# Moving one stretch of attention work by four matmuls, with its sums on VectorE in another order

## The chip, the cores and the metric

The kernel runs on one core of a Trainium2 chip. The metric is device time in microseconds (us) of one execution; lower is better. A core has TensorE (matrix products, PE in the profile; its weight loads are PEld), VectorE (DVE), ScalarE (ACT) and GpSimd (POOL), which each work through their own instructions in the order in which the program gives them, and SyncE (SP), on whose queue most DMA transfers are issued. The engines wait for one another through semaphores. TensorE writes only to PSUM, from where VectorE and ScalarE fetch its results.

## The reference

Retention (attention with a decay in place of the softmax) over 8 batches, 8 heads, 576 positions and 64 columns a head, and then a bilinear feed-forward layer on all 4608 tokens:

```python
scores = scale * np.matmul(q, k.transpose(0, 1, 3, 2))
Dmat = np.where(rel >= 0, gamma[:, None, None] ** rel[None, :, :], 0.0)
ret = scores * Dmat[None, :, :, :]
attn = np.matmul(ret, v)                       # (batch, head, position, 64)
x = attn.transpose(0, 2, 1, 3).reshape(B * S, H * D)   # 4608 x 512
a = x @ w_a                                    # 512 x 1536
b = x @ w_b
return (a * b @ w_out)                         # 4608 x 512
```

`rel` is query position minus key position, and `gamma` is one constant per head, so the decay factors into a power that belongs to the query and one that belongs to the key.

## The kernel before

**Attention as a recurrence.** The 576 positions of a batch are cut into nine blocks of 64. Within a block, the masked scores are multiplied with the values; what lies before the block comes through a state, the sum of key-times-value products of all earlier blocks. Most of the work is done in *pairs*: a pair is 256 positions (four blocks) of one batch, all heads. `PAIRS` lists them; the first eight are (batch 0, first 256), (1, first), (2, first), (0, second), (1, second), (2, second), (3, first), (3, second). The first three are made in another way at the start of the kernel (the `..._step` functions). The fourth pair has the number 3 and the fifth the number 4.

**A pair's steps.** `load_pair` (SP's queue) brings q, k and v. `ahead` (POOL) casts q and k to bf16 (`qkb`, L484 and L488) and multiplies v by the key's decay (`vb`, L495). `turn` (SP's queue, L507) transposes q and k by DMA into `qkT`. `stretch(into, outof)` then puts the products of two pairs on TensorE at one place:

- `open_outputs(outof)`: products of the states with the queries of pair `outof` into the PSUM tile `o` (L628), and a tiny ScalarE copy from `o` (`fence`, L671).
- `keyed(into, ...)`: keys times values of pair `into`, per block, into two PSUM tiles `kv` (L538).
- `matched(into)`: the scores of pair `into` into the PSUM tile `sc` (L600).
- `close_outputs(outof)`: masked scores times values, added into `o` (L641).

What follows these products on VectorE and ScalarE isn't issued on the spot. It is put into a list, `later`, as small entries:

- `add` (L560, L563, VectorE): the running sums of the blocks' `kv`, four in all. A pair whose number is in `SPLIT` has two entries of two sums each; any other pair has one entry with all four.
- `scaled` (L654, VectorE): the outputs times the query's decay, into `x`, two entries.
- `convert` and `convert_swapped` (ScalarE), each in one entry with half of the mask product `masked` (L609, VectorE): the sums become bf16 states (L570 for one block; L567 for the blocks whose halves are swapped, and, for the second pair of an odd batch, `left_states`).

**The feed-forward layer sets the order.** Tokens are taken in blocks of 512, 256, 256 and then 512. `ffn_block` runs, for each of the 12 parts F of the hidden width, four products into `pa` (L794), a ScalarE copy `ha` (L802), four products into `pb` (L809) and a VectorE product `hT` = ha x pb (L814). Then for each 128 tokens u it accumulates 12 products over F into an output tile `po` (L828), which is copied to `osb` (L837 on ScalarE in a block of 256 tokens) and stored. `pa`, `pb`, `po` and the `kv` tiles of a stretch share the tag "ab", which has four PSUM tiles.

`ffn_block` is a generator. After each product it yields that product's cost, where 512 columns count as 1, and whether other work may come in here (after each `hT`, after every fourth product of `po`, and after a `po` is copied). The loop at the end of the kernel adds the costs up and starts every entry of `todo` whose time has come:

```python
while todo and edge and at >= todo[0][0]:
    _, fn, args = todo.pop(0)
    fn(*args)
```

`ffn_block` also calls `pop()`, which issues the first entry of `later`: in a block of 256 tokens after each `hT`, after the products F = 2, 5 and 8 of a `po`, and after a `po` is copied. Whatever is left in `later` is issued by `flush()` at the end of a block, and at the start of the next stretch.

**Around the change.** The first block (512 tokens) counts 144 in all. The second, tokens 512 to 767, runs from 144 to 216: 48 for pa and pb, and 12 for each of its two output tiles. `stretch(3, None)` is due at 170 and `stretch(4, 3)`, with the scores of the fifth group and the outputs of the fourth, at 197. The third block, tokens 768 to 1023, reads the `x` that the fourth group's outputs give. At 200 and 200.1 to 200.3 `todo` also has `ahead(6)`, `turn(6)` and `load_pair(7)`. The buffers that pair 6 is cast and transposed into are those of pair 3 (three buffers each).

Of the kernel before, what the change touches and what calls it, by code (L numbers as in the profile page):

```python
# [18 lines left out]
def kernel(  # L19
# [25 lines left out]
    NP = NTOK // 256  # L45
    LEFT = {NP - 3: 0, NP - 1: 1}
    FIRST = 3
    SPLIT = (3, 5)
    assert S == 9 * 64 and B == 8

    PAIRS = [(0, 0), (1, 0), (2, 0), (0, 1), (1, 1), (2, 1)]
# [41 lines left out]
    def ps_next(name):  # L93

        opening.close()
        ps_o[0] = opening.enter_context(
            tc.tile_pool(name=name, bufs=1, space=PS))
# [179 lines left out]
    later = []  # L277
# [5 lines left out]
    def flush():  # L283
        while later:
            later.pop(0)()
# [235 lines left out]
    def keyed(n, alone):  # L521
# [64 lines left out]

        parts = [(0, 1), (2, 3)] if n in SPLIT else [(0, 1, 2, 3)]
        for part in parts:
# [3 lines left out]
    def matched(n):  # L592
        qkT = of(transposed, n)
        sc = ps_sc.tile([128, 2, HP, 2, 64], FP32, tag="sc", name="sc2")
        begun = Begun()
        for c in range(HP):
            for kp in (0, 1):
                for a, r in QUADS:
                    on = r ^ a
                    nc.tensor.matmul(sc[half(a), on, c, kp, :],  # L600
                                     qkT[half(on), 1, kp, c, half(a)],
                                     qkT[half(on), 0, kp, c, half(a)],
                                     start=begun.first(on, a), stop=True,
                                     skip_group_check=True)
        sT = st_pool.tile([128, 2, HP, 2, 64], BF16, tag="sT", name="sT2")
        scored[FIRST + n, "pair"] = sT

        def masked(on):
            nc.vector.tensor_tensor(  # L609
                sT[:, on].rearrange("p c k s -> p (c k) s"),  # L610
                sc[:, on].rearrange("p c k s -> p (c k) s"),
                mask3.unsqueeze(1).to_broadcast([128, 2 * HP, 64]),
                op=ALU.mult)
        return masked

    def from_states(n, o, begun):
        qkT = of(transposed, n)
        st = states_of.pop(n)
        first = first_of.pop(n, st[:, 0])
        for c in range(HP):  # L620
            for kp in (0, 1):
                for a, r in QUADS:
                    i = 2 * kp + a
                    if block_of(n, i) == 0:
                        continue
                    on = r ^ a
                    own = st[:, i] if i else first
                    nc.tensor.matmul(o[a][half(r), c, kp, :],  # L628
                                     own[half(on), c, :],
                                     qkT[half(on), 0, kp, c, half(a)],  # L630
                                     start=begun.first(a, r), stop=True,
                                     skip_group_check=True)

    def keys_into(n, o, begun):
        vb = of(natural, n)[1]
        sT = of(scored, n)
        for c in range(HP):
            for kp in (0, 1):
                for a, r in QUADS:
                    v0 = kp * DM + c * 128 + 64 * r  # L640
                    nc.tensor.matmul(o[half(r), a, c, kp, :],  # L641
                                     vb[half(a), v0:v0 + 64],
                                     sT[half(a), r ^ a, c, kp, :],
                                     start=begun.first(a, r), stop=True,
                                     skip_group_check=True)

    def scaling(n, o):

        s0 = 64 * block_of(n, 0)
        step = 0 if n in LEFT else 128  # L650

        def scaled(kp):
            t0 = place(n) * 256 + kp * 128
            nc.vector.tensor_tensor(  # L654
                x_of(t0, 128).rearrange("p c (a s) -> p c a s", a=2),
                o[:, :, :, kp].rearrange("p a c s -> p c a s"),
                qs[:, :, s0 + kp * step:s0 + kp * step + 128]
                .rearrange("p c (a s) -> p c a s", a=2),
                op=ALU.mult)
        return scaled  # L660
# [3 lines left out]
    def open_outputs(n):  # L664

        o = ps_o[0].tile([128, 2, HP, 2, 64], FP32, tag="o", name="o2")
        begun = Begun()
        from_states(n, [o[:, a] for a in (0, 1)], begun)

        kp = int(0 in (block_of(n, 0), block_of(n, 1)))  # L670
        nc.scalar.copy(fence, o[:, :, 0, kp, 0])  # L671
        opened[n] = o, begun

    def close_outputs(n):

        o, begun = opened.pop(n)
        keys_into(n, o, begun)
        scaled = scaling(n, o)
        later.append(lambda: scaled(0))
        later.append(lambda: scaled(1))  # L680
# [7 lines left out]
    def summing(n, own, of_keys):  # L688

        scaled = scaling(n, both.rearrange("p k a c s -> p a c k s"))  # L690

        def summed(kp):
            fresh = int(block_of(n, 2 * kp) == 0)
            for a in range(2):
                nc.scalar.copy(both[:, kp, a], of_keys[:, a, :, kp]
                               if a < fresh else own[a][:, :, kp])
            nc.vector.tensor_tensor(both[:, kp, fresh:], both[:, kp, fresh:],
                                    of_keys[:, fresh:, :, kp], op=ALU.add)
            scaled(kp)

        later.append(lambda: summed(0))
        later.append(lambda: summed(1))
# [11 lines left out]
    def stretch(into, outof):  # L714

        flush()
        if into == FIRST:
            ps_next("ps_pair")
        if into in LEFT:
            own = [ps_ffn.tile([128, HP, 2, 64], FP32, tag="ab", name=f"os{a}")  # L720
                   for a in (0, 1)]
            of_keys = ps_o[0].tile([128, 2, HP, 2, 64], FP32, tag="o",
                                   name="o2")
            from_states(outof, own, Begun())
            masked = matched(into)
            keys_into(outof, of_keys, Begun())
            summing(outof, own, of_keys)
            later.append(lambda: masked(0))
            later.append(lambda: masked(1))
            return  # L730
        if outof is not None:
            open_outputs(outof)
        convert, convert_swapped = keyed(into, outof is None)
        masked = matched(into)
        if outof is not None:
            close_outputs(outof)
        later.append(lambda: (convert(), masked(0)))
        later.append(lambda: (convert_swapped(), masked(1)))

# [244 lines left out]
    def third_turn():  # L984
        for i in (4, 5):
            transpose_step(i, (Q, "act"), (K, "dve"))

    todo = [(100, early_casts, ()),
            (112.1, cast_step, (5, Q, "act")),
            (124, third_turn, ()), (128, third_states, ()),  # L990
            (136, third_outputs, ())]
    todo += [(60 + 10 * n, total_of, (n,)) for n in (0, 1)]
    todo += [(136, total_of, (2,))]
    todo += [(28 + 6 * step, pair_tables, (step,)) for step in range(13)]
    todo += [(170, stretch, (3, None)), (197, stretch, (4, 3)),
             (252, stretch, (5, 4)), (274, open_alone, (5,)),
             (278, close_outputs, (5,)), (336, stretch, (6, None)),
             (372, stretch, (7, 6)), (408, stretch, (8, 7))]
    for n in range(8, NP, 2):
# [68 lines left out]
```

## Time and profile before

| what | value |
|---|---|
| median of 3 runs | 325.16 us (325.08 to 325.69) |
| the profiled execution | 325.43 us |
| its span in the profile | 323.7 us, 8631 instructions |
| granted TensorE clock | 1.00 |
| HBM read, written | 37.75 MB, 9.44 MB |
| chain that ended last | PE 92%, DMA 2%, SPq 2%, ACT 1%, issue 1%, DVE 1% |

A row of the time-ordered view gives the start in us from the beginning of the span, the duration, the engine, the line of the kernel, the operation, what it writes and reads, how many instructions are merged into the row, and in brackets how long the engine had been idle and what it had waited for. Matmul durations contain pipeline latency, so successive matmuls overlap; a few matmul records can be missing. "issue" is time in which an engine waited for nothing that the profile shows. The third block begins at 68.45 us, and the stretch of the change stands between 63.7 and 65.2 us.

### The profile page before, as it was taken

What the parts mean: (1) busy time and instruction counts of PE and PEld (TensorE: products, weight loads), DVE (VectorE), ACT (ScalarE), POOL (GpSimd) and SP (SyncE); (2) the same over time, 40 slices, a digit from 0 to 9 for tenths busy, and PEclk for the clock granted to TensorE, in tenths of its full rate; (3) what the DMA queues carried; (4) which work ended last, traced back from release to release, by engine and by line L of the source; (5) the groups of instructions that cost most, each with busy time, mean ns of one, the idle gap of its engine ahead of it and who ended that gap; (6) DMA issues with size and microseconds to landing.
All of it is one profiled execution on the core that took longest, in us unless ns stands there. A gap on an engine that the chain in (4) does not pass through costs nothing.

```text
span 323.7 us, 8631 instructions
## 1 busy us (share of the span) xinstructions
PE 314.0 (97%) x3573; PEld 164.4 (51%) x3611; DVE 165.4 (51%) x294; ACT 131.5 (41%) x293; POOL 118.8 (37%) x158
## 2 busy tenths in 40 slices
PE   7899999999999999999999999999999999999996
PEld 3564457778444554444454545454445444444444
DVE  5744445665546754835374626562566256514321
ACT  7735753463435523533253324442433343313321
POOL 4990077574755274447165305450530000000000
PEclk9999999999999999999999999999999999999999
DMA  8999999999999999999999169935840520031013
GB/s 216 255 196 207 259 231 189 200 176 206 174 221 223 195 208 206 269 222 263 175 197 216 52 163 198 207 74 144 194 86 19 104 76 2 2 97 32 1 23 108
DMA packets 145431, 50.90 MB, mean 157 GB/s; under 512 B 126704, under 2 KB 140912, under 8 KB 145392
## 3 DMA queue, kind: packets, MB, share of 16 engines
q1 hardware_dynamic: 140112, 45.37, 68.4%
q0 software_dynamic: 4752, 4.72, 8.8%
q8 instruction: 28, 0.46, 0.6%
q10 hardware_dynamic: 528, 0.26, 0.3%
q14 instruction: 11, 0.09, 0.1%
HBM read 37.75 MB, written 9.44 MB: 146 GB/s over the span
## 4 chain that ended last, share of the span: by engine, by line
PE 92%; DMA 2%; SPq 2%; ACT 1%; issue 1%; DVE 1%; DVEq 0%
PE pb L809 29%; PE po L828 29%; PE pa L794 28%; DMA qf<-in_q_dram 2%; SPq L159 2%; PE sc L600 1%; PE o L628 1%; PE o L641 1%; PE kv L538 1%; PE pa L771 1%; ACT state_after L386 0%; ACT vb L319 0%; PE tp L329 0%; DVE hT L814 0%; ACT own L390 0%
## 5 line engine op out<-in xcount | busy, mean ns | idle before, releaser
L814 DVE TENSOR_TENSOR hT<-ha,pb 128x512 bf16<-128x512 bf16 (+1 forms) x120 | 75.9, 633 | 94.8 <-PE pb L809 86.6
L802 ACT CAST ha<-pa 128x512 bf16<-128x512 f32 (+1 forms) x120 | 64.8, 543 | 115.9 <-PE pa L794 109.9
L809 PE MATMUL pb<-xT,wb_sb 128*128 128x512 bf16 (+1 forms) x474 | 111.2, 357 | 0.5
L794 PE MATMUL pa<-xT,wa_sb 128*128 128x512 bf16 (+1 forms) x452 | 106.9, 356 | 1.2 <-issue 0.6
L828 PE MATMUL po<-wo_sb,hT 128*128 128x512 bf16 (+2 forms) x442 | 94.7, 367 | 1.7 <-issue 1.4
L809 PEld LDWEIGHTS <-wb_sb 128*128 128x128 bf16 x480 | 47.0, 98 | 46.6 <-issue 0.3
L794 PEld LDWEIGHTS <-wa_sb 128*128 128x128 bf16 x468 | 45.0, 98 | 44.4 <-issue 0.2
L828 PEld LDWEIGHTS <-hT 128*128 128x128 bf16 x456 | 42.7, 98 | 47.2
L484 POOL CAST qkb<-qf 64x1024 bf16<-64x1024 f32 x15 | 15.5, 1031 | 64.4 <-DMA qf<-in_q_dram 55.1
L495 POOL TENSOR_TENSOR vb<-vf,vs 128x1024 bf16<-128x1024 f32 (+1 forms) x17 | 28.9, 1700 | 13.3 <-DMA vf<-in_v_dram 6.1
L839 DVE COPY osb<-po 128x512 f32<-128x512 f32 (+2 forms) x17 | 11.1, 653 | 43.0 <-PE po L828 43.0
L837 ACT COPY osb<-po 128x512 f32<-128x512 f32 (+1 forms) x21 | 12.0, 573 | 43.4 <-PE po L828 40.5
L484 POOL CAST qkb<-kf 64x1024 bf16<-64x1024 f32 (+1 forms) x17 | 16.4, 966 | 16.7 <-DMA kf<-in_k_dram 16.5
L563 DVE TENSOR_TENSOR sums<-kv,sums 128x256 f32<-128x256 f32 x44 | 18.7, 424 | 2.8 <-PE kv L538 0.8
L609 DVE TENSOR_TENSOR sT<-sc,mask 128x512 bf16<-128x512 f32 x30 | 19.4, 681 | 0.0
L488 POOL CAST qkb<-kf 64x512 bf16<-64x512 f32 (+1 forms) x34 | 18.7, 579 | 1.0
L488 POOL CAST qkb<-qf 64x512 bf16<-64x512 f32 x30 | 17.6, 615 | 0.6
L567 ACT CAST states<-sums 64x512 bf16<-64x512 f32 x26 | 16.0, 617 | 0.3
L654 DVE TENSOR_TENSOR xT<-o,qs 128x512 bf16<-128x512 f32 x24 | 15.4, 682 | 1.5 <-PE o L641 1.5
L311 POOL CAST qkb<-kf 128x512 bf16<-128x512 f32 x5 | 3.1, 617 | 16.9 <-DMA kf<-in_k_dram 16.9
L355 DVE TENSOR_TENSOR sT<-sc,mask_s 128x1024 bf16<-128x1024 f32 x6 | 7.2, 1222 | 1.3 <-PE sc L347 1.2
L855 PE MATMUL w<-ones 128*128 128x512 bf16 x17 | 6.3, 482 | 1.5 <-DVE idxp_f L204 1.5
(88 smaller groups left out, 163.5 us busy)
## 6 DMA issues: line engine op xcount, KB each, us to landing
qf<-in_q_dram SPq DMA_DIRECT2D x32, 256.0 KB, 4.7
vf<-in_v_dram SPq DMA_DIRECT2D x32, 256.0 KB, 5.2
kf<-in_k_dram SPq DMA_DIRECT2D x31, 256.0 KB, 4.8
out_dram<-osb SPq DMA_DIRECT2D x25, 256.0 KB, 3.2
out_dram<-osb SPq DMA_DIRECT2D x21, 128.0 KB, 2.6
wo_sb<-in_moe_w_out_dram POOLq DMA_DIRECT2D x3, 512.0 KB, 16.7
qf<-in_q_dram SPq DMA_DIRECT2D x8, 128.0 KB, 3.2
kf<-in_k_dram SPq DMA_DIRECT2D x8, 128.0 KB, 3.5
```

The costliest lines, as they stand in the source:

```text
L484: nc.gpsimd.tensor_copy(qkb[0:64, w, e], t[0:64, e])
L488: nc.gpsimd.tensor_copy(to[:, :, 1 - r], fro[:, :, r])
L495: nc.gpsimd.tensor_tensor(vb[:, e].rearrange("p (h d) -> p h d", d=D), t[:, e].rearrange("p (h d) -> p h d", d=D), decay[:, at], op=ALU.mult)
L563: nc.vector.tensor_tensor(sums[:, i], own, prev, op=ALU.add)
L567: nc.scalar.copy(to(half(1 - r)), fro(half(r)))
L609: nc.vector.tensor_tensor(sT[:, on].rearrange("p c k s -> p (c k) s"), sc[:, on].rearrange("p c k s -> p (c k) s"), mask3.unsqueeze(1).to_ ...
L654: nc.vector.tensor_tensor(x_of(t0, 128).rearrange("p c (a s) -> p c a s", a=2), o[:, :, :, kp].rearrange("p a c s -> p c a s"), qs[:, :, s ...
L794: nc.tensor.matmul(pa[:, 0:n], wa_sb[:, c, fs], xT[:, c], start=(c == 0), stop=(c == NC - 1))
L802: nc.scalar.copy(ha[:, 0:n], pa[:, 0:n])
L809: nc.tensor.matmul(pb[:, 0:n], wb_sb[:, c, fs], xT[:, c], start=(c == 0), stop=(c == NC - 1))
L814: nc.vector.tensor_tensor(hT[:, F, 0:n], has[F][:, 0:n], pb[:, 0:n], op=ALU.mult)
L828: nc.tensor.matmul(po[:, 0:width], hT[:, F, u * 128:(u + 1) * 128], wo_sb[:, F, cols], start=(F == 0), stop=(F == NF - 1))
```

## The change

`stretch(4, 3)` is due at 201 in place of 197, four products of 512 columns later. Pair 4 is added to `SPLIT`, so that its four state sums are two entries in place of one, and in that stretch the second of them is taken out of its place in the list and put behind the two `scaled` entries. `later` then reads: sums 0 and 1, scaled 0, scaled 1, sums 2 and 3, convert with half of the mask, convert_swapped with the other half. No instruction is added or left out.

```diff
-    SPLIT = (3, 5)
+    SPLIT = (3, 4, 5)
@@ stretch(into, outof)
         masked = matched(into)
         if outof is not None:
             close_outputs(outof)
+        if into == 4:
+            later.append(later.pop(1))
         later.append(lambda: (convert(), masked(0)))
         later.append(lambda: (convert_swapped(), masked(1)))
@@ todo
-    todo += [(170, stretch, (3, None)), (197, stretch, (4, 3)),
+    todo += [(170, stretch, (3, None)), (201, stretch, (4, 3)),
              (252, stretch, (5, 4)), (274, open_alone, (5,)),
```

## The prediction

> **What bounds the kernel now.** I began with the page's table of engines, then took the waits of TensorE from 60 to 130 us, and then the order-of-time view of TensorE, ScalarE and VectorE around the stretch that moves. In the first, TensorE (PE) is busy for 97% of the span. In the second, it waits there for no other engine: all that stands ahead of its matmuls is 0.7 us of "issue".
>
> ```profile
> PE 314.0 (97%) x3573; PEld 164.4 (51%) x3611; DVE 165.4 (51%) x294; ACT 131.5 (41%) x293; POOL 118.8 (37%) x158
> ```
>
> ```profile
> PE po L828 <- issue: 0.5, 3, 0.2
> PE pa L794 <- issue: 0.2, 1, 0.2
> ```
>
> So a delay of TensorE in this part goes to the end whole, and there is next to no wait here that a reordering could take away. Next, TensorE in order of time (start, duration, line, operation). The stretch is the rows before 65.21; the block of tokens 768 to 1023 begins at 68.45 with pa, pb, pa, pb, pa, 0.44 us each.
>
> ```profile
> 64.00 0.44 PE L538 MATMUL kv<-vb,qkb 64*64 64x64 bf16 x32
> ...
> 64.58 0.47 PE L641 MATMUL o<-sT,vb 64*64 64x64 bf16 x32
> 65.21 3.40 PE L828 MATMUL po<-wo_sb,hT 128*128 128x512 bf16 x15 [0.16 <-issue]
> 68.45 0.60 PE L794 MATMUL pa<-xT,wa_sb 128*128 128x256 bf16 x4
> 68.88 0.60 PE L809 MATMUL pb<-xT,wb_sb 128*128 128x256 bf16 x4
> 69.32 0.60 PE L794 MATMUL pa<-xT,wa_sb 128*128 128x256 bf16 x4
> 69.76 0.60 PE L809 MATMUL pb<-xT,wb_sb 128*128 128x256 bf16 x4
> 70.19 0.60 PE L794 MATMUL pa<-xT,wa_sb 128*128 128x256 bf16 x4
> ```
>
> The rows of ScalarE (ACT) and of VectorE (DVE) over the same time:
>
> ```profile
> 64.24 0.16 ACT L671 COPY fence<-o 128x2 f32<-128x2 f32 x1 [0.97 <-PE o L628]
> 66.06 0.59 ACT L837 COPY osb<-po 128x512 f32<-128x512 f32 x1 [1.66 <-PE po L828]
> 66.67 0.41 ACT L570 CAST states<-sums 128x256 bf16<-128x256 f32 x1
> 67.08 1.25 ACT L567 CAST states<-sums 64x512 bf16<-64x512 f32 x2
> 68.34 0.82 ACT L567 CAST left_states<-sums 64x256 bf16<-64x256 f32 x2
> 69.06 0.57 ACT L837 COPY osb<-po 128x512 f32<-128x512 f32 x1
> 69.54 0.84 ACT L802 CAST ha<-pa 128x256 bf16<-128x256 f32 x2
> ```
>
> ```profile
> 64.59 0.42 DVE L563 TENSOR_TENSOR sums<-kv,own 128x256 f32<-128x256 f32 x1 [0.87 <-PE kv L538]
> 65.12 1.34 DVE L563 TENSOR_TENSOR sums<-kv,sums 128x256 f32<-128x256 f32 x3
> 66.38 1.28 DVE L654 TENSOR_TENSOR xT<-o,qs 128x512 bf16<-128x512 f32 x2
> 67.58 1.28 DVE L609 TENSOR_TENSOR sT<-sc,mask 128x512 bf16<-128x512 f32 x2
> 69.94 0.95 DVE L814 TENSOR_TENSOR hT<-ha,pb 128x256 bf16<-128x256 bf16 x2 [1.08 <-PE pa L794]
> ```
>
> The reader is to see that ScalarE ran without a pause from 66.06 to 70.38. The state casts (L570, L567) lie between the copies of the two output tiles. The second copy starts at 69.06 though its matmuls were through by 68.65; the first ha cast is therefore late too, at 69.54, and ends at 69.91. The tag "ab" has four PSUM tiles. When the third pa starts at 70.19, the two pa and two pb before it hold all four, so it needs the first ha cast finished. It was, by 0.28 us.
>
> **Part 1, the place.** The schedule counts a product of 512 columns as 1. This block starts at 144, its twelve pa/pb pairs cost 48, its output tiles 12 each, and work is let in after every fourth product of a tile. So 197 is reached at 200, after eight products of the first tile, and 201 at 204, after its twelfth and its copy. A product takes (68.45 - 65.21) / 15 = 0.216 us, so on TensorE the four products come 0.86 us earlier and the stretch 0.86 us later. Its work is unchanged (129 small matmuls in 1.3 us in that window), and so is the gap beside it, since it follows a 512-column product both times: zero, with bounds of -0.58 us (both 0.42 us before its first load and 0.16 us after it vanish) and +0.58 us (one more of each).
>
> The eight moved-up products need their hT. The last hT of the block ends at 63.72 and its product would start at 64.27: covered by 0.55 us.
>
> **Part 2, the queue of small steps.** The list that the loop drains decides the rest. Before: sums, scale, scale, cast+mask, cast+mask, five entries; the five places left in the two tiles (one after the ninth product, one after the tile, three in the second) took them all. After: six entries (two sums, scale, scale, the other two sums, cast+mask, cast+mask), and only four places are left (three within the second tile and one behind its copy). They take the sums, the scales and the other sums. Both cast+mask entries go out at the block's end, behind the second tile's copy and ahead of the next block's first ha cast.
>
> **VectorE.** The first sum starts 0.86 later, 65.45; two sums at 0.45 end at 66.36; the scales run 66.38 to 67.66, just as before, as they need the last L641 product (65.05 + 0.86 = 65.91). So the next block's x is ready at 67.7 for 68.45. The other two sums end at 68.6 and the masks at 69.9. Both kv tiles come free at 68.1 and 68.6, ahead of the second pa at 69.32. Cost nothing; cover 0.75 us at x. If that went and x came at 68.6 (all four sums first), pa would start 0.15 us later, which the wait below swallows.
>
> **ScalarE.** The first tile's copy starts 0.41 us after its last product's start (65.64 to 66.06): now 64.27 + 0.41 = 64.68, ending at 65.27. The fence copy (0.16) comes behind it, to 65.43; the L641 products, which write the tile that it reads, are due at 64.58 + 0.86 = 65.44. Between 0 and 0.1 us of TensorE; I take 0.
>
> The second copy: its last product starts at 68.23, the copy at 68.65. Then, start to start as in the rows: copy to first cast 0.61, L570 0.41, the L567 pair 1.26, the left_states pair 0.72 to whatever follows. First ha cast at 68.65 + 3.00 = 71.65, done at 71.65 + 0.37 = 72.02, against 69.91 before. The third pa can start at about 72.06 instead of 70.19: **TensorE stands still for 1.87 us**. Behind it, the first hT product runs 72.05 to 72.47 and the fourth buffer turn (pb at 72.50) just fits; the next ones have 0.4 us to spare. So no second wait follows. TensorE never waits for a transfer or an engine from here to 130 us beyond issue, so nothing gives it back.
>
> [...] In the rows two casts of one kind follow each other without overlap (67.08 to 68.34 is 2 x 0.617 plus 0.02), and only at a change between casts and PSUM copies does one start 0.10 us early (68.34 + 0.82 = 69.16 against 69.06). [...]
>
> Bounds from rows: if all six starts were 0.10 early, durations of 0.59 + 0.41 + 1.23 + 0.81 = 3.04 less 0.60 give 2.44 and a wait of 1.31. If TensorE hid nothing, all 2.39 us of casts (66.67 to 69.06) plus 0.1 for the fence count: 2.5. I take 1.87, which is the same instructions in the same order.
>
> **Part 3, other queues.** Pair 6's casts (POOL) are now written ahead of the stretch, as are its transposes (SP), and the loads of pair 7. The stretch issues nothing on POOL or SP, so both queues keep their order. Casts and transposes reuse buffers that the stretch reads last, by 65.91. The casts start at 78.24 (their q loads are issued at 73.39, 4.7 us to landing), the transposes at 84.59: cover 12 us and 18 us. Zero; if it went, POOL, and SP with pair 7's v load behind the transposes, would start late by as much, and the first to feel it would be the score products that read pair 6 from 97.44.
>
> **Sum.** +1.87, taken as +1.9. The profiled execution took 325.43 us (span 323.7 and 1.7 around it), 0.27 over the median of 325.16. It becomes 327.3, the median 327.1.
>
> **Rivals.**
> *Casts in time (not slower).* The same list, but the cast entries reach ScalarE before the second tile's copy. To cost nothing the first ha cast must end by 70.15, so the casts must start by 67.4 rather than 69.26. For it: sums and data are ready (the sums that the first cast needs end at 66.36), and ScalarE idles from 65.4 to 68.6. Against it: no place is left to let them in, and in all rows ScalarE keeps the written order. Time 325.2, or 324.6 if the 0.58 us of issue goes as well.
> *The clock falls after the pause.* The first eight warm-up matmuls of 512 columns take 0.42 us each rather than 0.216:
>
> ```profile
> 1.52 3.34 PE L855 MATMUL w<-ones 128*128 128x512 bf16 x8 [1.52 <-DVE idxp_f L204]
> ```
>
> so TensorE can run at half rate after standing still, though the granted clock reads 1.00 there. If 1.9 us were enough, 3.3 us at half rate would cost 1.6 more: 328.7. Against it: after the 0.46 us wait at 11.42 the spacing is 0.21 again, but no pause between that and the launch is seen in the trace, so the rows leave the point open. [...]
>
> **How the numbers follow.** ScalarE's casts stall TensorE: 0.87, own range 326.4 to 327.9 (median plus 1.3 to 2.5, and 0.1 to 0.2 for the runs' spread). Casts in time: 0.08, of which 0.02 below 324.5. Clock falls: 0.05. 0.2%, 0.65 us, is about what a measurement can tell here. Slower 0.87 + 0.05 = 0.92; within 0.06; faster 0.02. The range 326.4 to 327.9 is the likeliest case's own; its tails and the other cases leave out about 0.2.
>
> **What would show it.** Right: the stretch's L628 follows the twelfth product; the second L837 copy at about 68.65, L570 and the L567 casts behind it, the first ha at 71.65; a wait of about 1.9 us ahead of the third pa on "ACT ha", and all later rows of TensorE that much later; scale rows (L654) unmoved at 66.4. Wrong: L567 rows ahead of the second L837, or ha at 69.5 (then no change); product spacing of 0.42 after the pause (then the clock); or a wait ahead of the first pa on "DVE xT" (then VectorE).

## The result and the profile after

The changed kernel takes 327.05 us in the median (326.81 to 327.35, 5 runs) against 325.16 (325.04 to 325.69, 5 runs): a ratio of 1.0057, with a 95% interval of 1.0043 to 1.0070. The ratios leave out slow executions, of which there is one here, the 332.67 us of `pause_half`. The change makes the kernel slower by 1.9 us, within 0.05 us of the forecast. The profiled execution took 327.35 us, with a span of 325.6 against 323.7.

The waits of TensorE in the changed kernel, between 60 and 130 us (who waited for whom: us in total, times, longest), have one entry that wasn't there before:

```profile
PE pa L796 <- ACT ha L804: 1.7, 1, 1.7
```

TensorE in order of time (start, duration, line; from line 737 on, lines stand two higher than in the kernel before):

```profile
61.92 2.75 PE L830 MATMUL po<-wo_sb,hT 128*128 128x512 bf16 x12
...
65.45 0.47 PE L641 MATMUL o<-sT,vb 64*64 64x64 bf16 x32
65.85 2.76 PE L830 MATMUL po<-wo_sb,hT 128*128 128x512 bf16 x12
68.45 0.60 PE L796 MATMUL pa<-xT,wa_sb 128*128 128x256 bf16 x4
68.89 0.60 PE L811 MATMUL pb<-xT,wb_sb 128*128 128x256 bf16 x4
69.33 0.60 PE L796 MATMUL pa<-xT,wa_sb 128*128 128x256 bf16 x4
69.76 0.60 PE L811 MATMUL pb<-xT,wb_sb 128*128 128x256 bf16 x4
72.07 0.60 PE L796 MATMUL pa<-xT,wa_sb 128*128 128x256 bf16 x4 [1.71 <-ACT ha L804]
72.50 0.60 PE L811 MATMUL pb<-xT,wb_sb 128*128 128x256 bf16 x4
```

The stretch now stands between two output tiles of twelve products each. The next block starts at 68.45, as before. Then the third pa starts at 72.07 in place of 70.19, 1.88 us late. The wait shows as 1.71 because it is counted from the modelled end of the last matmul. ScalarE over the same time:

```profile
64.71 0.59 ACT L839 COPY osb<-po 128x512 f32<-128x512 f32 x1 [1.43 <-PE po L830]
65.19 0.17 ACT L671 COPY fence<-o 128x2 f32<-128x2 f32 x1
68.66 0.59 ACT L839 COPY osb<-po 128x512 f32<-128x512 f32 x1 [3.30 <-PE po L830]
69.27 0.41 ACT L570 CAST states<-sums 128x256 bf16<-128x256 f32 x1
69.68 1.24 ACT L567 CAST states<-sums 64x512 bf16<-64x512 f32 x2
70.94 0.82 ACT L567 CAST left_states<-sums 64x256 bf16<-64x256 f32 x2
71.66 0.63 ACT L804 CAST ha<-pa 128x256 bf16<-128x256 f32 x2
```

ScalarE now idles for 3.3 us ahead of the second copy, and then has the state casts in front of the first ha cast, which moves from 69.54 to 71.66. VectorE did what the change asks of it:

```profile
65.46 0.42 DVE L563 TENSOR_TENSOR sums<-kv,own 128x256 f32<-128x256 f32 x1 [1.73 <-PE kv L538]
65.99 0.42 DVE L563 TENSOR_TENSOR sums<-kv,sums 128x256 f32<-128x256 f32 x1
66.33 1.28 DVE L654 TENSOR_TENSOR xT<-o,qs 128x512 bf16<-128x512 f32 x2
67.53 0.87 DVE L563 TENSOR_TENSOR sums<-kv,sums 128x256 f32<-128x256 f32 x2
```

The scales start at 66.33, where they stood before (66.38), so x is there for the first pa. The 1.9 us stay to the end: the later stretch whose first key products stood at 97.44 has them at 99.31.

### The profile page after: what moved, and what is told of

The parts are those of the page before. It is cut to its first block, busy times and chain, and to the rows that moved or that the text cites. A ratio compares the mean times of both kernels' runs of the same rounds, so it can differ in the third digit from the quotient of the medians.

```text
span 325.6 us, 8668 instructions
## 1 busy us (share of the span) xinstructions
PE 318.2 (98%) x3611; PEld 164.9 (51%) x3611; DVE 165.1 (51%) x294; ACT 131.5 (40%) x293; POOL 118.6 (36%) x158
## 4 chain that ended last, share of the span: by engine, by line
PE 93%; DMA 2%; SPq 2%; ACT 1%; issue 1%; DVE 1%; DVEq 0%
PE po L830 29%; PE pb L811 28%; PE pa L796 28%; DMA qf<-in_q_dram 2%; SPq L159 2%; PE sc L600 1%; PE o L641 1%; PE o L628 1%; PE kv L538 1%; PE pa L773 1%; PE o L437 0%; PE sc L347 0%; PE kv L374 0%; ACT states L567 0%; PE tp L329 0%
## 5 line engine op out<-in xcount | busy, mean ns | idle before, releaser
L796 PE MATMUL pa<-xT,wa_sb 128*128 128x512 bf16 (+1 forms) x468 | 108.8, 357 | 1.7 <-ACT ha L804 1.7
L830 PE MATMUL po<-wo_sb,hT 128*128 128x512 bf16 (+2 forms) x456 | 97.0, 368 | 0.0
L567 ACT CAST states<-sums 64x512 bf16<-64x512 f32 x26 | 16.0, 617 | 0.3
L857 PE MATMUL w<-ones 128*128 128x512 bf16 x19 | 7.2, 503 | 1.5 <-DVE idxp_f L204 1.5
```

The costliest lines, as they stand in the source:

```text
L567: nc.scalar.copy(to(half(1 - r)), fro(half(r)))
L796: nc.tensor.matmul(pa[:, 0:n], wa_sb[:, c, fs], xT[:, c], start=(c == 0), stop=(c == NC - 1))
L830: nc.tensor.matmul(po[:, 0:width], hT[:, F, u * 128:(u + 1) * 128], wo_sb[:, F, cols], start=(F == 0), stop=(F == NF - 1))
```

## The experiments

The theory: the whole loss is the state casts that ScalarE gets behind the second output tile's copy, since TensorE runs into the first ha cast when the four shared PSUM tiles are full. The rivals: the later place costs by itself (everything from the stretch on is 0.86 us late); the new order on VectorE costs; TensorE waits for something other than the tiles; or the clock falls after the pause. Differences below are medians against the kernel before in the same series (325.31, 325.18 and 325.10 us in the three series).

### One half of the change, and the other

The new order alone, at the old place:

```diff
-    todo += [(170, stretch, (3, None)), (201, stretch, (4, 3)),
+    todo += [(170, stretch, (3, None)), (197, stretch, (4, 3)),
```

> The changed kernel with the stretch back at 197: only the split sums and the new order on VectorE stay. Theory (what counts is which casts ScalarE gets behind the second output tile's copy): six entries for five places, so the swapped casts (1.26 + 0.72 us) go out at the block's end, behind the copy, while the L570 cast (0.41) still goes ahead of it. First ha cast at 68.66 + 0.60 + 1.26 + 0.72 = 71.24, done at 71.61, third pa at 71.65: +1.46 us, 326.6. Rival 'the later place itself costs' (everything 0.86 us late): as before, 325.2. Rival 'the new order on VectorE costs it all': as the changed kernel, 327.05.

Measured: 326.76 us, +1.45, ratio 1.0043 (1.0031 to 1.0055). ScalarE, in order of time (this execution runs 0.42 us earlier throughout than the one of the kernel before):

```profile
66.25 0.40 ACT L570 CAST states<-sums 128x256 bf16<-128x256 f32 x1
68.23 0.59 ACT L839 COPY osb<-po 128x512 f32<-128x512 f32 x1 [1.57 <-PE po L830]
68.84 1.24 ACT L567 CAST states<-sums 64x512 bf16<-64x512 f32 x2
70.09 0.82 ACT L567 CAST left_states<-sums 64x256 bf16<-64x256 f32 x2
70.82 0.63 ACT L804 CAST ha<-pa 128x256 bf16<-128x256 f32 x2
```

L570 slips in ahead of the copy, the L567 casts don't. With the place unchanged, three quarters of the 1.9 us are lost: six entries find only five places ahead of the second tile's copy, and the sixth, with the L567 casts, goes out behind it. This run holds the split and the new order together; that the sixth entry matters and not the order is read from the rows of ScalarE.

The new place alone, with the old entries and the old order:

```diff
-    todo += [(170, stretch, (3, None)), (197, stretch, (4, 3)),
+    todo += [(170, stretch, (3, None)), (201, stretch, (4, 3)),
```

> The kernel before with the stretch at 201: the old five entries and the old order on VectorE. Theory: five entries for four places; L570 goes out behind the second tile's copy and the swapped casts at the block's end, so ScalarE has the same rows as in the changed kernel and the first ha cast ends at 72.03. The four sums now stand ahead of the scales, x is ready at 68.53 instead of 67.6 and the first pa starts at about 68.57 instead of 68.45, which the later wait swallows: +1.9 us, 327.05. Rival 'VectorE's new order costs it': 325.2 to 325.3. Rival 'both waits add up': 327.2 or more.

Measured: 327.39 us, +2.1, ratio 1.0068 (1.0053 to 1.0082). The scales on VectorE, and then TensorE, in order of time:

```profile
67.26 1.28 DVE L654 TENSOR_TENSOR xT<-o,qs 128x512 bf16<-128x512 f32 x2
```

```profile
68.59 0.60 PE L794 MATMUL pa<-xT,wa_sb 128*128 128x256 bf16 x4
...
72.08 0.60 PE L794 MATMUL pa<-xT,wa_sb 128*128 128x256 bf16 x4 [1.58 <-ACT ha L802]
```

The first pa is 0.14 us late, right behind the scales that end at 68.54, and the third pa starts at 72.08, as in the changed kernel (72.07). The median alone would also fit the rival by which both waits add up (327.2 or more). The rows speak against it: the later stretch has its first key products at 99.32, against 99.31 in the changed kernel. So the delay of x is swallowed here, and the new order on VectorE gains nothing as long as ScalarE sets the time. The halves don't add up (1.45 and 2.1 against 1.9): both act through the same row, the first ha cast.

### The same place without the late casts

Here the six steps are joined so that all of them find a place within the second output tile. First with the new order on VectorE:

```diff
         if into == 4:
-            later.append(later.pop(1))
+            steps = [later[i] for i in (0, 2, 3, 1)]
+            later[:] = [lambda: (steps[0](), steps[1]()),
+                        lambda: (steps[2](), steps[3]()),
+                        lambda: (convert(), masked(0),
+                                 convert_swapped(), masked(1))]
+            return
```

> The changed kernel at 201 with its order on VectorE, but with the six steps joined into three entries (sums and first scale; second scale and sums; all casts and masks), so that all of it is let in within the second tile and ScalarE has the casts ahead of the second copy. Theory: the swapped casts now wait for the third sum (ends at about 67.97) and run from 68.0 to 70.0, the copy ends at 70.55, and the second pb, which needs the tile that this copy frees, waits from 69.76 to about 70.6: +0.85 us, 326.0, with the wait on the osb copy in place of the ha cast. Rival 'the later place itself costs': 327.05.

Measured: 326.15 us, +0.84, ratio 1.0027 (1.0018 to 1.0036). The wait has changed its place, as expected. The waits of TensorE, then ScalarE (this execution too runs about 0.35 us early):

```profile
PE pb L816 <- ACT osb L844: 0.7, 1, 0.7
```

```profile
66.10 0.41 ACT L570 CAST states<-sums 128x256 bf16<-128x256 f32 x1 [1.10 <-DVE sums L563]
67.63 1.25 ACT L567 CAST states<-sums 64x512 bf16<-64x512 f32 x2 [1.12 <-DVE sums L563]
68.89 0.82 ACT L567 CAST left_states<-sums 64x256 bf16<-64x256 f32 x2
69.61 0.57 ACT L844 COPY osb<-po 128x512 f32<-128x512 f32 x1
```

Now the scales stand in the way: the swapped casts wait 1.12 us for the sums that were put behind them, and push the copy back. Then with the four sums first, from the kernel before:

```diff
-    todo += [(170, stretch, (3, None)), (197, stretch, (4, 3)),
+    todo += [(170, stretch, (3, None)), (201, stretch, (4, 3)),
@@ stretch
+        if into == 4:
+            steps = list(later)
+            later[:] = [steps[0], lambda: (steps[1](), steps[2]()),
+                        lambda: (convert(), masked(0),
+                                 convert_swapped(), masked(1))]
+            return
```

> The stretch at 201, all four sums ahead of the scales as in the kernel before, and three entries (sums; both scales; all casts and masks), let in within the second tile. Theory: the third sum ends at about 66.87, the swapped casts run from 66.9 to 69.0 ahead of the second copy (68.9), the first ha cast ends at 69.75, the third pa finds its tile free. Only x is late, by 0.1 us at the first pa: +0.1 us, 325.3, no wait on ScalarE. Rival 'the later place itself costs': 326 or more.

Measured: 325.40 us, +0.09, ratio 1.0007 (0.9996 to 1.0017). There is no wait of TensorE in the view from 60 to 130 us, and ScalarE has its casts ahead of the copy again:

```profile
66.86 1.24 ACT L567 CAST states<-sums 64x512 bf16<-64x512 f32 x2
68.12 0.82 ACT L567 CAST left_states<-sums 64x256 bf16<-64x256 f32 x2
68.84 0.57 ACT L843 COPY osb<-po 128x512 f32<-128x512 f32 x1
69.32 0.36 ACT L808 CAST ha<-pa 128x256 bf16<-128x256 f32 x1
```

So the later place hardly costs anything by itself: with the same place, the same products and the casts ahead of the copy, 0.09 us of the loss is left (by the interval, at most 0.55), about what the late x was expected to cost. That rival has fallen.

### The casts later still

```diff
-        flush()
+        if tb != 1:
+            flush()
         tok += n
```

> The changed kernel without the flush at the end of the block of tokens 512 to 767: the two cast+mask entries stay in the list and are let in after the first and the second hT of the next block. Theory: ScalarE casts the first ha at 69.25, then L570, the second ha, the swapped casts (70.4 to 72.4) and only then the third ha, which ends at about 72.8; the fifth pa, which needs that tile, waits from 71.94 to about 72.8: +0.9 us, 326.1, no wait at the third pa. Rival 'the late casts cost the same wherever they stand': 327.05. Rival 'the later place itself costs': 327.05.

Measured: 326.17 us, +0.99, ratio 1.0028 (1.0016 to 1.0040). The third pa doesn't wait; the fifth does, behind the same casts (this execution runs 0.15 us early):

```profile
72.65 0.60 PE L796 MATMUL pa<-xT,wa_sb 128*128 128x256 bf16 x4 [0.70 <-ACT ha L804]
```

So the same casts cost half as much there. What they cost depends on which ha cast they stand in front of, and on the tiles that TensorE can still fill by then, not on their sum.

### More tiles

If TensorE stops because the four shared tiles are full, two more move the stop on by one pa and one pb. The first try takes the two halves of the idle output tile:

```diff
+                if tb == 2 and F == 2:
+                    extra = ps_o[0].tile([128, 2, 512], FP32, tag="o",
+                                         name="extra")
                 pa = (begun[F] if tb == 0 and F in begun else
+                      extra[:, 0] if tb == 2 and F == 2 else
...
+                pb = (extra[:, 1] if tb == 2 and F == 2 else
```

> The changed kernel, but in the block of tokens 768 to 1023 the third pa and the third pb take the two banks of the output tile o, which nothing uses from 67.6 us to the next stretch, in place of two of the four shared tiles. ScalarE's queue is unchanged, its first ha cast still ends at 72.03. Theory (TensorE stops because all four shared PSUM tiles are held until that cast): the third pa runs at 70.19 and the third pb at 70.63 without a wait, and the fourth pa is the one that waits, from 71.07 to 72.07: +1.0 us in place of +1.9, 326.2. Rival 'TensorE waits for ScalarE or the masks for another reason than the tiles' (the x, the hT buffer): the third pa still starts at 72.07, 327.05.

Measured: 327.28 us, +2.1, ratio 1.0061 (1.0046 to 1.0076): a miss by 1.1 us. TensorE, and then the ScalarE cast that it waits for, in order of time (about 0.36 us early throughout):

```profile
69.84 0.60 PE L800 MATMUL extra<-xT,wa_sb 128*128 128x256 bf16 x4
72.25 0.60 PE L816 MATMUL extra<-xT,wb_sb 128*128 128x256 bf16 x4 [1.81 <-ACT ha L808]
```

```profile
71.83 0.37 ACT L808 CAST ha<-extra 128x256 bf16<-128x256 f32 x1
```

The third pa ran without a wait, as the theory has it. But the third pb then waited for ScalarE's read of the other half of the same tile: the wait had only moved on. Why the write into one half waited 1.81 us for the read of the other no run shows. With two separate tiles:

```diff
+                if tb == 2 and F == 2:
+                    third_a = ps_o[0].tile([128, 2, 512], FP32, tag="o",
+                                           name="third_a")
+                    third_b = ps_sc.tile([128, 2, 512], FP32, tag="sc",
+                                         name="third_b")
...
+                      third_a[:, 0] if tb == 2 and F == 2 else
...
+                pb = (third_b[:, 0] if tb == 2 and F == 2 else
```

> The changed kernel with the third pa of the block of tokens 768 to 1023 in the output tile o and the third pb in the score tile sc, two tiles in place of the two halves of one (in fifth_tile the third pa did run without a wait, but the third pb waited for ScalarE's read of the other half). The score tile is read for the last time at 69.6. Theory (TensorE stops when the shared tiles are all held until the first ha cast at 72.03): the third pa and pb run at 70.19 and 70.63, the fourth pa waits from 71.07 to 72.07: +1.0 us, 326.2. Rival (something other than the number of free tiles holds the products back): 327.05 to 327.3.

Measured: 326.33 us, +1.2, ratio 1.0030 (1.0012 to 1.0048), where +1.0 was expected. TensorE, in order of time (about 0.2 us early):

```profile
70.44 0.60 PE L818 MATMUL third_b<-xT,wb_sb 128*128 128x256 bf16 x4
71.87 0.60 PE L802 MATMUL pa<-xT,wa_sb 128*128 128x256 bf16 x4 [0.84 <-ACT ha L810]
```

Both run without a wait, and the fourth pa would have started 0.44 us after the third pb, at 70.88; it is 0.99 us late, as expected of the tiles. ScalarE's queue has the same rows in the same order, so the number of free tiles is shown to set where TensorE stops.

### Does the clock fall after a pause?

The prediction had left open whether a pause of 1.9 us drops TensorE's clock. A pair of casts done again makes it longer, by 0.62 us (one of the pair again), 1.25 (the pair twice in all) or 3.75 (four times). The edit of `pause_1`; `pause_3` has 3 in place of 1, and `pause_half` one ScalarE copy in place of the loop:

```diff
             swapped(lambda r: odd_ones(into, r, 1),
                     lambda r: odd_ones(sums, r, 0))
+            for _ in range(1 if n == 4 else 0):
+                swapped(lambda r: odd_ones(into, r, 1),
+                        lambda r: odd_ones(sums, r, 0))
```

> The changed kernel with the pair of 64x512 casts of the swapped states done twice (the same values written again), 1.25 us more on ScalarE at that place. Theory: the third pa starts at 73.3, TensorE pauses for 3.0 us by the waits, 328.3. If the clock holds, the pa and pb after the pause take 0.44 us per four matmuls from the first on; rival 'the clock falls after a pause': 0.85 us per four for a while, and up to 1.6 us more, 329.9.

> As before, with the pair of casts done four times, 3.75 us more on ScalarE. Theory: the third pa starts at 75.8, TensorE pauses for 5.5 us, 330.8 if the clock holds. [...]

> The changed kernel with one of the two 64x512 casts of the swapped states done twice: 0.62 us more on ScalarE, a pause of TensorE of 2.3 us. If the clock holds through such a pause: 327.7 in all runs, granted clock 1.00. If it can fall there as in the runs of pause_1 with a granted clock of 0.99: some runs 1.2 us or more above 327.7.

> pause_1 once more, for the share of executions in which the clock falls after a pause of 3.0 us: 328.3 to 328.7 where the granted clock stays at 1.00, 329.8 and more where it reads 0.995 or less. [...]

The pause is that of the profiled execution.

| kernel | pause by the waits | median, ratio (95% interval) | execution times, with the granted clock over the span |
|---|---|---|---|
| changed | 1.7 us | 327.05, 1.0057 (1.0043 to 1.0070) | 326.81 to 327.35, all five at 0.999 to 1.00 |
| pause_half | 2.25 us | 329.75, 1.0108 (1.0068 to 1.0148) | 327.69 and 327.90 at 1.00; 329.57, 329.93, 330.00 at 0.995; 332.67 at 0.99 |
| pause_1 | 3.0 us | 329.92, 1.0150 (1.0111 to 1.0189) | 328.66 at 1.00; 329.82 and 330.01 at 0.995; 332.91 at 0.99 |
| pause_1_again | 3.0 us | 330.41, 1.0158 (1.0112 to 1.0205) | 328.69 and 329.32 at 1.00; 329.90 and 330.92 at 0.995; 331.98 and 333.09 at 0.99 |
| pause_3 | 5.6 us | 334.01, 1.0275 (1.0249 to 1.0301) | 333.66 to 334.08 at 0.99; 336.01 at 0.985 |

Where the clock held, pause_half meets its 327.7, and pause_1 and its repeat come within 0.4 us of the 328.3 that the longer queue gives, but for one execution of 329.32. Most executions lie above, and those have the lower clock. So four of six executions of pause_half took 1.8 us or more above 327.7, as in the second of its two cases, and in the repeat of pause_1 four of six lie at 329.8 or more, all with a clock of 0.995 or less, as its expectation has it for such a clock. pause_3 was 2.9 us or more above the 330.8 of a clock that holds. The windows of its profiled execution show the reason (stretch in us; length, and PE's busy time first, and the granted clock third from the end):

```profile
73.00:76.00 3.00, 0.00 (x0) 0.00 (x0) 0.00 (x0) 2.90 (x5) 0.70 (x1) 0.97 1.02 214
76.00:78.00 2.00, 0.00 (x0) 0.00 (x0) 0.00 (x0) 1.94 (x5) 0.32 (x1) 0.50 1.27 228
78.00:80.00 2.00, 1.57 (x8) 1.11 (x8) 0.75 (x2) 1.02 (x4) 1.88 (x3) 0.50 1.35 217
80.00:82.00 2.00, 2.00 (x11) 1.35 (x10) 0.42 (x1) 0.37 (x1) 1.88 (x3) 0.50 1.34 224
82.00:84.00 2.00, 2.00 (x17) 1.66 (x16) 0.84 (x2) 0.65 (x2) 0.43 (x2) 0.84 1.05 178
```

The clock is halved at about 75.8 (0.97 over 3 us is 0.18 us at half) and comes back at about 82.6 (0.84 over 2 us). From 78.43, where TensorE resumes, that is 4.2 us at half rate, a loss of 2.1 us beside the 3.75 of the longer pause. The two come to 5.85 on top of 327.05, 332.9. The profiled execution, at 336.01, had fallen once before, ahead of the pause: its granted clock is 0.50 from 18 to 20 us, and its third block begins at 70.96 in place of 68.45, 2.5 us late. The other three, at 333.66 and more, lie 0.8 us or more above 332.9; the reason stays open. In pause_1_again the matmuls after a 3.0 us pause are spaced twice as wide as usual:

```profile
76.47 1.01 PE L799 MATMUL pa<-xT,wa_sb 128*128 128x256 bf16 x4 [3.00 <-ACT ha L807]
77.28 1.06 PE L814 MATMUL pb<-xT,wb_sb 128*128 128x256 bf16 x4
78.13 1.06 PE L799 MATMUL pa<-xT,wa_sb 128*128 128x256 bf16 x4
```

They are 0.81 to 0.85 us apart, against 0.43 to 0.44 in the changed kernel from 72.07 on. The four groups behind the pause take 3.27 us (76.47 to 79.74) in place of 1.75, a loss of 1.5 us. The profiled execution of pause_1, with the same pause of 3.0 us, held its clock at 1.00. So 3.0 us can drop the clock and need not.

That profiled execution of pause_1_again, too, had fallen once before its pause:

```profile
18.00:20.00 2.00, 2.00 (x12) 1.49 (x11) 0.63 (x2) 0.32 (x2) 2.00 (x4) 0.54 1.07 162
20.00:22.00 2.00, 2.00 (x13) 1.47 (x12) 0.00 (x0) 0.09 (x1) 1.88 (x6) 0.60 1.18 189
```

Its third block begins at 71.56, 3.0 us later than in the profiled execution of pause_1 (68.56). The two falls account for its time: 328.66 + 3.0 + 1.5 = 333.2, against 333.09. TensorE waited 1.07 us between short matmuls shortly before, until 15.88; whether this was the cause is not shown.

A fall at 18 us can't come from a pause at 73 us, so the table counts falls of two kinds. A clock of 0.995 over the span doesn't tell them apart: one of 16 executions of the kernel before, in the last series, has it too, and took 328.09, 3.0 us over the median, though that kernel has no such pause. The executions of pause_1 at 0.995 lie 1.2 to 1.4 us above the one at 1.00, which is nearer to the 1.5 of a fall behind the pause. Those of pause_half lie 1.7 to 2.3 above its two at 1.00, between 1.5 and 3.0, and the only traced execution of that kernel held its clock through the 2.25 us. So whether 2.25 us is enough stays open.

What the counts do show is that longer pauses and falls go together: one of the 127 executions of kernels with pauses of at most 1.8 us has a granted clock of 0.995 or less, and 15 of the 20 of kernels with longer ones. Why some of these falls come early is not known.

## Why the prediction was right

- **The place.** As forecast, the stretch follows the twelfth product, TensorE's work is the same, and the products that moved up didn't wait: all twelve of the tile follow from 61.92 on, 0.216 us apart. (They are four; the prediction says eight in one place.) The gap bound of 0.58 us was too wide for a reason of its own: the 0.16 us "issue" at 65.21 stood for one missing matmul record. The row has 15 records of 16, and it starts 0.63 us after the L641 row, in place of 0.40 in the changed kernel (65.45 to 65.85), one product more.
- **The list.** Four places for six entries, both cast entries behind the second copy. (The count for 197 leaves out a sixth place, behind the second copy, which five entries did not need.) This is shown by the rows of ScalarE, and by the two runs that change only the entries and get the loss down to +0.84 and +0.09.
- **VectorE.** Sums at 65.46 (forecast 65.45), scales at 66.33 (66.38), covered. The other sums and the masks ended at 68.40 and 69.60, 0.2 and 0.3 us ahead of the forecast, and nothing hung on them. The forecast that a late x would be swallowed is shown by the run with the place alone: first pa 0.14 us late, third pa at the same time.
- **ScalarE.** Second copy 68.66 (68.65), first ha 71.66 (71.65), third pa 72.07 (72.06). The fence was worth nothing: L641 at 65.45 against 65.44. The start-to-start times of the rows before, taken over unchanged, carried the number. The two L567 casts from `sums` did not overlap here either (69.68 to 70.94 is 2 x 0.62 and 0.02). Other casts did, by 0.10 us: the first ha cast starts at 71.66 while the casts before it end at 71.76, and the two ha casts, of 0.36 to 0.37 us each, take 0.63. Two casts from `sums` can overlap too: later in the same execution one (L572) starts at 101.95, while the one ahead of it (L570) ends at 102.05. So it is too general when the prediction says that two casts of one kind follow each other without overlap; its sum used start-to-start times and didn't depend on it. What decides whether they overlap is not shown.
- **The four tiles.** That the third pa is the one that stops, because of the tiles, is shown by two_tiles.
- **The other queues.** Pair 6's casts on POOL start at 79.38 in place of 78.24, and wait there for their q load; TensorE waits for none of it.
- **The rivals.** "Casts in time" did not happen, but the kernel with three entries shows that it was the right counter-case: it takes 325.40. "The clock falls" did not happen either (granted 1.00 around the pause, 0.44 us spacing at once). Its chance was set at 0.05. No run shows the 3.3 us at half rate that it reckons with after a pause of 1.9 us; the warm-up row beside it is 3.34 us long, and behind the longer pauses the half rate lasted 4.2 us in pause_3, and in pause_1_again four groups took 3.27 us in place of 1.75. The clock was halved about 2.7 us into the pause of pause_1_again (0.55 over 76 to 78 us, after the last matmul's end at 73.46), and 2.9 us into that of pause_3. How near the pause of 1.7 us came to one that drops the clock is open. That the clock would hold was the weakest step of the prediction, and in part it was luck.

## What to carry to other kernels

When work is moved later in a kernel whose side steps are drained from a list at fixed places, count the places that are left: what finds none is issued in a lump, and its cost is set by what stands behind it on its engine. Here 2.4 us of casts were free ahead of a copy and cost 1.9 us behind it, and reordering another engine didn't help. Start-to-start times from the rows of the same instructions, put behind one another, gave the wait to 0.01 us; the tiles that the bottleneck engine can still fill say when it starts.

## What the runs showed of the hardware

Pauses of TensorE of 1.6 to 1.8 us left its clock at 0.999 or 1.00 over the span in all 17 executions of three kernels (the changed one, the place alone, and the two halves of one tile). After a pause of 3.0 us one traced execution went on at half rate (pause_1_again) and another at full rate (pause_1); after 5.6 us the traced one went on at half rate for 4.2 us, so the fall outlasted the pause in both. With 2.25 us four of six executions, with 3.0 us seven of ten, and with 5.6 us all four had a granted clock of 0.995 or less over the span. Two of the traced executions (pause_1_again and pause_3) also show a fall at 18 to 22 us, ahead of the pause, and for 2.25 us no trace shows one behind it. On ScalarE, the changed kernel's two L567 casts from `sums` at 69.68 did not overlap, while the ha cast at 71.66 and an L572 cast from `sums` at 101.95 started 0.10 us before the end of the one ahead. And the eight warm-up matmuls of 512 columns at the start are spaced 0.42 us apart, against 0.216 for the products of 512 columns at 61.92, while the granted clock reads 1.00 from 0 to 6 us; no run shows why.
